# One attention and gated feed-forward kernel: a unit's scores and its attention outputs each gathered in one place, and the keys of batch 1 turned by a DMA

## The chip, the core and the metric

The kernel runs on one core of a Trainium2 chip, in one launch. The core has five engines with queues of their own: PE (TensorE, the matmuls; PEld are its weight loads), DVE (VectorE), ACT (ScalarE), POOL (GpSimd) and SP (SyncE, which only issues DMAs here). POOL issues DMAs too: those that convert float32 to bfloat16 on the way. The metric is the device time of one execution in microseconds (us), as the median of several runs; lower is better.

## The reference, cut to what matters

Two layers follow each other. The first is attention in which a query sees the keys closer than 16 positions and, beside them, 24 block summaries: the maximum over 32 keys and the mean over 32 values.

```python
batch, n_heads, seq, head_dim = (4, 8, 768, 64)
block, window = (32, 16)
k_sum = k.reshape(B, H, nb, block, D).max(axis=3)
v_sum = v.reshape(B, H, nb, block, D).mean(axis=3)
mask_l = np.abs(pos[:, None] - pos[None, :]) < window
scores_l = where(mask_l, scale * q @ k.T, -1e9)
scores_s = scale * q @ k_sum.T + log(block)
a = softmax(concat([scores_l, scores_s]))
attn = a @ concat([v, v_sum])
```

The second is a gated feed-forward layer on the 3072 rows of 512 that come out, with 1536 hidden columns:

```python
ffn_out = (gelu(x @ w_gate) * (x @ w_val)) @ w_out
out = x + sigmoid(x @ w_res) * ffn_out
```

## The kernel before, in words

The order of all instructions is written out by hand; each engine runs its own in that order, and semaphores are put in where data passes between engines or a buffer is used again.

**Units.** The work is cut into NU = 8 units u of 384 rows: batch b = u // 2, half = u % 2. The 8 heads go in 4 pairs hp. A unit has 6 tiles t of 64 queries; a tile's 64 + 32 neighbouring keys and the 24 block maxima stand side by side as 128 columns of `kW`, so that one 64-row matmul per tile and head gives all its scores, keys on the partitions. The two heads of a pair lie on the upper and lower 64 partitions, so their matmuls run two at a time.

**Attention of a unit.** `s_step` (L322) makes 12 score matmuls of a pair into two banks of PSUM (L317), takes the exponent on ACT into a tile `P` (L337 when both banks come from the two-bank pool `ps_s`, else twice L334), and from unit 1 on multiplies by the mask on DVE (L341). `av_step` (L347) makes the 12 matmuls with the values (L355) into an `ao` bank, whose row sums come along as a 65th column; `av_end` (L371) divides on DVE (a reciprocal, L373, and a product, L375, into `xn`). `xn` is then turned into `xT`: by PE and a copy in the first two units (`xt_step`, L377), by a DMA transpose from SP for each of four column groups ko from unit 2 on (`xt_dma`, L384).

**Feed-forward of a unit.** For each of 12 blocks fo, `fo_step` (L406) has PE make `g` and `vv` (four matmuls each, L395), ACT the gelu (L400) and DVE the product `gvT` (L401). `fo_first` (L413) leaves ko = 3 of both to the end, so that the last turned group may come late; `fo_last_two` (L420) makes both `g` before both `vv`. Then for each of 3 row groups `res_step` (L429: four matmuls, L433, and a tanh), `ffn_step` (L438: twelve matmuls, L443) and `end_step` (L458: two DVE passes, L449 and L452, and a store from SP, L456).

**Where the two meet.** `first_out` (after unit 0) and `mid_out` (L616, after units 1 to 6) interleave the end of unit u with the attention of unit n = u + 1. `mid_out` has: scores of pairs 0 and 1; two `res_step`; 4 of 12 matmuls of `f` 0; values of pairs 0 and 1; scores of pairs 2 and 3; the other 8 matmuls of `f` 0 and 3 of `f` 1; values of pairs 2 and 3; the rest. So PE goes from large matmuls to 64-row score matmuls or 64-column value matmuls and back twice, and the score and value groups also follow each other directly once.

**PSUM.** Eight banks: `ps_mm` has four, taken in turn by `g`, `vv`, `r`, `f` and some score banks; `ps_s` two; `ps_t` and `ps_o` one each.

**Keys, queries and values of a batch.** Batch 0 has a path of its own. For batches 2 and 3, `load_k_nat` (L118) loads k by eight DMAs from POOL with rows on the partitions, `turn_k` (L130) turns all of it by one DMA transpose from SP into `kW`, `k_rims` (L243) copies the 32 neighbouring keys of each tile on POOL, and `k_blocks` (L234) makes the block maxima on DVE, one pair after each of the steps fo = 2 to 5 of the unit before. For batch 1, k comes by one DMA into `k_sb` (L89) and is turned on PE: `turn_all` (L227) makes 64 small transposes (L220) after step fo = 0 of unit 1, and `k_place` (L251) after fo = 0, 2, 4 and 6 copies a pair on ACT (L252) and makes its maxima and rims on DVE. In POOL's queue the loads of a batch stand as k, then v (`v_loads`, L105, eight DMAs), then q (`load_q_nat`, L125, six). SP turns q in two halves (`turn_q`, L134), of which the first serves the batch's first unit. `vsum_grp` (L286) sums blocks of values with 12 PE matmuls (L290), a copy on ACT and four small DMAs from POOL; POOL then spreads the means (`vsum_bc`, L299). For batch 1 it stands after step fo = 5 of unit 1. `v_rims` (L110) copies neighbouring values by two DMAs from SP.

Of the kernel before, what the change touches and what calls it, by code (L numbers as in the profile page):

```python
# [8 lines left out]
F32 = mybir.dt.float32  # L9
BF16 = mybir.dt.bfloat16  # L10
# [5 lines left out]
def kernel(  # L16
# [11 lines left out]
    nc = tc.nc  # L28
# [25 lines left out]
    wpool = ctx.enter_context(tc.tile_pool(name="wpool", bufs=1))  # L54
    qk = ctx.enter_context(tc.tile_pool(name="qk", bufs=1))
    work = ctx.enter_context(tc.tile_pool(name="work", bufs=3))
    ppool = ctx.enter_context(tc.tile_pool(name="ppool", bufs=4))
    upool = ctx.enter_context(tc.tile_pool(name="upool", bufs=2))
    ps_mm = ctx.enter_context(tc.tile_pool(name="ps_mm", bufs=4, space=bass.MemoryType.PSUM))
    ps_s = ctx.enter_context(tc.tile_pool(name="ps_s", bufs=1, space=bass.MemoryType.PSUM))  # L60
# [17 lines left out]
    q_nat = const.tile([128, NQ, DM], BF16, name="q_nat")  # L78
    vext = [const.tile([128, NT, H, VP], BF16, name=f"vext{i}") for i in range(2)]
    vsum = [const.tile([128, DM], BF16, name=f"vsum{i}") for i in range(2)]  # L80
    vpart = const.tile([128, DM], BF16, name="vpart")
    w_gate = wpool.tile([128, KO, DFF], BF16, name="w_gate")
    w_val = wpool.tile([128, KO, DFF], BF16, name="w_val")
# [55 lines left out]
    with tc.manual_schedule():  # L139
# [182 lines left out]
        def s_step(u, hp, st, banks=None, tiles=None):  # L322
            if tiles:
                s, banks = tiles, True
            elif banks:
                s = [p.tile([128, 512], F32, tag=tag, name="s") for p, tag in banks]
            else:
                s2 = ps_s.tile([128, 2, 512], F32, tag="s", name="s")
                s = [s2[:, hh] for hh in range(2)]
            s_mm(u, hp, [x[:, 0:TU] for x in s])  # L330
            P = ppool.tile([128, 2, HT, QT], BF16, tag="P", name="P")
            if banks:
                for hh in range(2):
                    nc.scalar.activation(P[:, hh].rearrange("p t q -> p (t q)"), s[hh][:, 0:TU], AF.Exp,  # L334
                                         scale=scale, bias=bias_t[:])
            else:
                nc.scalar.activation(P.rearrange("p a t q -> p a (t q)"), s2[:, :, 0:TU], AF.Exp,  # L337
                                     scale=scale, bias=bias_t[:])
            if u:
                Pf = P.rearrange("p a t q -> p (a t) q")  # L340
                nc.vector.tensor_mul(Pf, Pf, maskt.unsqueeze(1).to_broadcast([128, 2 * HT, QT]))  # L341
            st["P", hp] = P

        MM2 = ((ps_mm, "mm"),) * 2
        TO2 = ((ps_t, "t"), (ps_o, "ao"))
# [31 lines left out]
        def xt_step(u, ko, st, pool, tag, copy=nc.vector.tensor_copy):  # L377
            xp = pool.tile([128, TU], BF16, tag=tag, name="xp")
            for sub in range(NSUB):
                nc.tensor.transpose(xp[:, sub * 128:(sub + 1) * 128],  # L380
                                    st["xn"][:, ko, sub, :], ident[:])
            copy(st["xT"][:, ko, :], xp[:])

        def xt_dma(ko, st):  # L384
            nc.sync.dma_start_transpose(out=st["xT"][:, ko].rearrange("d (s k) -> d s k", k=128),
                                        in_=st["xn"][:, ko].rearrange("p s d -> p (s d)"))
# [6 lines left out]
        def gv_mm(ps, w, st, fo, kos):  # L393
            for ko in kos:
                nc.tensor.matmul(ps[:, 0:TU], w[:, ko, fo * 128:(fo + 1) * 128], st["xT"][:, ko, :],  # L395
                                 start=(ko == 0), stop=(ko == KO - 1), skip_group_check=True)

        def gv_end(gvT, fo, g, vv):
            ge = work.tile([128, TU], F32, tag="ge", name="ge")
            nc.scalar.activation(ge[:], g[:, 0:TU], AF.Gelu)  # L400
            nc.vector.tensor_mul(gvT[:, fo, :], ge[:], vv[:, 0:TU])  # L401

        def mm_tile(name):
            return ps_mm.tile([128, 512], F32, tag="mm", name=name)
# [13 lines left out]
            gv_end(gvT, 0, g, vv)  # L418

        def fo_last_two(st, gvT):  # L420
            g = [mm_tile("g"), mm_tile("g")]
            for i in range(2):
                gv_mm(g[i], w_gate, st, FO - 2 + i, range(KO))
            for i in range(2):
                vv = mm_tile("vv")
                gv_mm(vv, w_val, st, FO - 2 + i, range(KO))
                gv_end(gvT, FO - 2 + i, g[i], vv)

        def res_step(st, sub):  # L429
            ss = slice(sub * 128, (sub + 1) * 128)  # L430
# [117 lines left out]
        xt_step(0, 2, st, **t_turn)  # L548
        gv_part(0, 1)
        gv_mm(gv[1][0], w_gate, st, 1, (0, 1))  # L550
        xt_step(0, 3, st, **o_turn)
        gv_part(0, 2)
        gv_mm(gv[1][1], w_val, st, 1, (0, 1))
        gv_part(0, 3)
# [27 lines left out]
        def pool_after(x):  # L582
            nc.gpsimd.tensor_copy(gate2[:], x)
# [31 lines left out]

        def mid_out(u, st, gvT, nst):  # L616
            n = u + 1
            other = dict(pool=ps_t, tag="t")
            s_step(n, 0, nst)
            s_step(n, 1, nst, TO2)  # L620
            res_step(st, 0)
            res_step(st, 1)
            ffn_step(st, gvT, 0, 0, 4)
            av_step(n, 0, nst)
            xt_dma(0, nst)
            av_step(n, 1, nst, **other)
            xt_dma(1, nst)
            s_step(n, 2, nst)
            s_step(n, 3, nst, MM2)
            if n % 2 == 0:  # L630
                pool_after(nst["P", 3][0:1, 0, 0, 0:1])
                for i in range(2, 4):
                    vsum_bc(n // 2, 3 * i, 3 * i + 3, nc.gpsimd)
            ffn_step(st, gvT, 0, 4, FO)
            ffn_step(st, gvT, 1, 0, 3)
            av_step(n, 2, nst)
            xt_dma(2, nst)
            av_step(n, 3, nst, **other)
            xt_dma(3, nst)
            end_step(u, st, 0)  # L640
            ffn_step(st, gvT, 1, 3, FO)
            res_step(st, 2)
            end_step(u, st, 1)
            ffn_step(st, gvT, 2, 0, FO)
            end_step(u, st, 2)
# [9 lines left out]
        for u in range(NU):  # L655
            b, half = u // 2, u % 2
            nb = b + 1
            if half == 0 and nb == 1:
                k_sb[nb] = k_tile()
                load_k(nb, k_sb[nb], 0, 1)  # L660
                v_loads(nb)
                load_q_nat(nb)
            if u:
                gvT = upool.tile([128, FO, TU], BF16, tag="gvT", name="gvT")
            for fo in range(0 if u else 2, FO):
                if u == 0 and fo == 2:
# [24 lines left out]
                if half == 1 and nb < B:  # L691
                    if fo == 0:
                        v_rims(nb, 0, HT)
                        if nb > 1:
                            pool_after(st["xT"][0:1, KO - 1, 0:1])
                            load_q_nat(nb)
                    if fo == (5 if nb == 1 else 1):
                        turn_q(nb, 0)
                        turn_q(nb, 1)
                        vsum_grp(nb, ps_t, "t")  # L700
                        for i in range(2):
                            vsum_bc(nb, 3 * i, 3 * i + 3, nc.gpsimd)
                    if nb == 1:
                        if fo == 0:
                            tk = turn_all(k_sb[nb])
                        if fo in (0, 2, 4, 6):
                            hp = (2, 0, 1, 3)[fo // 2]
                            k_place(nb, hp, tk[hp])
                    elif 2 <= fo < 2 + NP:
                        k_blocks(nb, fo - 2)  # L710
            if u == NU - 1:
                last_out(u, st, gvT)
            else:
                nst = new_unit()
                (mid_out if u else first_out)(u, st, gvT, nst)
                st = nst

# [29 lines left out]
```

The softmax here doesn't subtract the row's maximum and nothing guards it: scores larger than these inputs give would overflow.

## Time and profile before

| what | value |
|---|---|
| median of 4 runs | 256.31 us (256.27 to 256.33) |
| the profiled execution | 256.28 us |
| span of its trace | 254.5 us |
| outside the span | 1.8 us |
| granted TensorE clock | 0.998 |
| `mid_out` of unit 2 in the trace, from the first score matmul to the next unit's first `g` | 98.04 to 110.63 us |

The profile is one execution. Its page gives each engine's busy time and share of the span, the chain of work that ended last (followed back from the last instruction, at each step to what released it), and groups of instructions by line, with what ended the idle time before them. The trace behind it also answers for a window of time: the chain in order, an engine's instructions (the timeline), or the instructions of one tile with the time from a DMA's issue to its landing. Times of matmuls in the chain are from the end of one to the end of the next; in the timeline they begin when the matmul begins. Now and then a matmul's record is missing.

### The profile page before, as it was taken

To read this page: it belongs to the slowest core of one execution; us is meant where nothing else is said; L and a number is where in the kernel's file an instruction comes from. 1 tells how busy PE (TensorE), PEld (TensorE's weight loads), DVE (VectorE), ACT (ScalarE), POOL (GpSimd) and SP (SyncE) were. 2 spreads that over 40 slices of the span, in tenths; PEclk is the share of its full clock that TensorE was granted. 3 is DMA by queue.
4 is the path that set the end of the run, shared out by engine and by line. 5 is a ranking of instruction groups with operands and counts; after the bars stand their busy time and mean duration, and the time that the engine had idled before them with its cause. 6 is when DMAs were issued, how large, how long until landed. Compare 5 with 4: busy or idle time off the path is not lost.

```text
span 254.5 us, 5847 instructions
## 1 busy us (share of the span) xinstructions
PE 246.3 (97%) x2303; PEld 139.6 (55%) x2328; DVE 158.7 (62%) x364; ACT 129.5 (51%) x216; POOL 97.1 (38%) x128
## 2 busy tenths in 40 slices
PE   6999999999999999999999999999999999999994
PEld 2676555565545655445545665445545665456544
DVE  6985796398667544858567544858567544854424
ACT  8885458366572337354572337354572337353320
POOL 8885542361606970374406970274404000000000
PEclk9999999999999999999999999999999999999999
DMA  5999999999404999289404999289604400230003
GB/s 80 177 181 197 197 205 207 175 176 221 64 19 120 156 149 161 50 148 183 105 18 117 167 158 148 49 151 175 109 18 117 96 3 0 50 139 0 3 1 124
DMA packets 98108, 29.34 MB, mean 115 GB/s; under 512 B 83225, under 2 KB 94945, under 8 KB 97985
## 3 DMA queue, kind: packets, MB, share of 16 engines
q0 software_dynamic: 68352, 14.76, 65.4%
q1 hardware_dynamic: 29728, 14.21, 24.5%
q8 instruction: 18, 0.29, 0.5%
q14 instruction: 10, 0.07, 0.1%
HBM read 29.36 MB, written 6.29 MB: 140 GB/s over the span
## 4 chain that ended last, share of the span: by engine, by line
PE 93%; DVE 5%; issue 2%; DVEq 0%
PE g L395 25%; PE vv L395 24%; PE f L443 23%; PE r L433 8%; PE s L317 3%; PE ao L355 3%; PE vs L282 1%; PE ao L367 1%; PE tp L220 1%; PE vs L290 1%; DVE ks L237 1%; PE xp L380 1%; DVE o L452 1%; DVE th L449 1%; PE gv L395 1%
## 5 line engine op out<-in xcount | busy, mean ns | idle before, releaser
L401 DVE TENSOR_TENSOR gvT<-ge,vv 128x384 bf16<-128x384 f32 x95 | 52.2, 552 | 48.1 <-PE vv L395 43.9
L400 ACT ACTIVATE ge<-g 128x384 f32<-128x384 f32 x95 | 46.6, 490 | 67.4 <-DVE gvT L401 34.8
L395 PE MATMUL g<-xT,w_gate 128*128 128x384 bf16 x380 | 78.0, 326 | 0.0
L395 PE MATMUL vv<-xT,w_val 128*128 128x384 bf16 x380 | 77.8, 326 | 0.0
L443 PE MATMUL f<-w_out,gvT 128*128 128x512 bf16 x262 | 62.7, 379 | 1.5 <-issue 1.1
L395 PEld LDWEIGHTS <-w_gate 128*128 128x128 bf16 x384 | 37.1, 98 | 26.2 <-issue 1.4
L395 PEld LDWEIGHTS <-w_val 128*128 128x128 bf16 x384 | 37.6, 98 | 24.7
L443 PEld LDWEIGHTS <-gvT 128*128 128x128 bf16 x276 | 25.7, 98 | 29.5
L107 POOL DMA_DIRECT2D vext<-in_v_dram x32 | 24.1, 778 | 16.1 <-DMA w_out<-in_moe_w_out_dram 5.6
L436 ACT ACTIVATE th<-r 128x512 f32<-128x512 f32 x24 | 13.5, 606 | 27.5 <-PE r L433 27.5
L449 DVE SCALAR_TENSOR_TENSOR th<-th,f 128x512 f32<-128x512 f32 (+2 forms) x26 | 16.6, 640 | 14.3 <-PE f L443 14.3
L433 PE MATMUL r<-w_res,xT 128*128 128x512 bf16 x88 | 22.7, 380 | 0.4
L341 DVE TENSOR_TENSOR P<-P,maskt 128x768 bf16<-128x768 bf16 x28 | 15.7, 562 | 11.2 <-ACT P L337 6.1
L302 POOL COPY vext<-vsum 32x1536 bf16<-32x1536 bf16 x12 | 17.2, 1463 | 12.1 <-DMA vsum<-vpart 12.0
L452 DVE SCALAR_TENSOR_TENSOR o<-th,xn 128x512 f32<-128x512 f32 (+2 forms) x26 | 18.2, 700 | 0.9
L375 DVE TENSOR_TENSOR xn<-ao,rz 128x384 bf16<-128x384 f32 x32 | 17.8, 558 | 1.1
L337 ACT ACTIVATE P<-s,bias_t 128x768 bf16<-128x768 f32 x17 | 15.3, 901 | 4.5 <-PE s L317 4.3
L127 POOL DMA_DIRECT2D q_nat<-in_q_dram x18 | 15.8, 905 | 0.9 <-issue 0.9
L334 ACT ACTIVATE P<-s,bias_t 128x384 bf16<-128x384 f32 x30 | 15.7, 579 | 0.0
L237 DVE TENSOR_REDUCE ks<-kW 128x24 bf16<-128x768 bf16 x16 | 15.1, 943 | 0.0
L433 PEld LDWEIGHTS <-xT 128*128 128x128 bf16 x96 | 8.8, 98 | 9.9
L373 DVE RECIPROCAL rz<-ao 128x6 f32<-128x6 f32 x32 | 6.1, 191 | 11.2 <-PE ao L355 10.3
(90 smaller groups left out, 186.5 us busy)
## 6 DMA issues: line engine op xcount, KB each, us to landing
out_dram<-o SPq DMA_DIRECT2D x23, 256.0 KB, 2.2
vext<-in_v_dram POOLq DMA_DIRECT2D x32, 96.0 KB, 6.6
q_nat<-in_q_dram POOLq DMA_DIRECT2D x18, 128.0 KB, 6.2
w_gate<-in_moe_w_gate_dram POOLq DMA_DIRECT2D x6, 256.0 KB, 8.7
w_val<-in_moe_w_val_dram POOLq DMA_DIRECT2D x6, 256.0 KB, 9.0
w_out<-in_moe_w_out_dram POOLq DMA_DIRECT2D x3, 512.0 KB, 14.3
k_nat<-in_k_dram POOLq DMA_DIRECT2D x16, 96.0 KB, 5.7
vext<-vext SPq DMA_DIRECT2D x6, 144.0 KB, 5.5
```

The lines of the kernel that those rows point to most:

```text
L107: nc.gpsimd.dma_start(out=vext[b % 2][0:QT, :, h, 0:D], in_=v[b, h].rearrange("(t p) d -> p t d", p=QT))
L127: nc.gpsimd.dma_start(out=q_nat[:, c].rearrange("p (h d) -> p h d", d=D), in_=q[b, :, c * 128:(c + 1) * 128, :].rearrange("h p d -> p h d"))
L237: nc.vector.tensor_reduce(out=ks.rearrange("d (t n) -> d t n", n=2), in_=kw[:, :, 0:QT].rearrange("d t (n w) -> d t n w", w=BLK), axis=myb ...
L302: eng.tensor_copy(vext[b % 2][96:128, lo:hi, :, 0:D], src)
L375: nc.vector.tensor_mul(xn, ao[:, :, :, 0:D], rz.to_broadcast([128, NSUB, 2, D]))
L395: nc.tensor.matmul(ps[:, 0:TU], w[:, ko, fo * 128:(fo + 1) * 128], st["xT"][:, ko, :], start=(ko == 0), stop=(ko == KO - 1), skip_group_ch ...
L400: nc.scalar.activation(ge[:], g[:, 0:TU], AF.Gelu)
L401: nc.vector.tensor_mul(gvT[:, fo, :], ge[:], vv[:, 0:TU])
L433: nc.tensor.matmul(r[:], st["xT"][:, ko, ss], w_res[:, ko, :], start=(ko == 0), stop=(ko == KO - 1))
L443: nc.tensor.matmul(st["f", sub][:], gvT[:, fo, ss], w_out[:, fo, :], start=(fo == 0), stop=(fo == FO - 1), skip_group_check=True)
L449: nc.vector.scalar_tensor_tensor(th[:, cs], th[:, cs], 1.0, f[:, 0:n], ALU.add, ALU.mult)
L452: nc.vector.scalar_tensor_tensor(o.rearrange("p (k d) -> p k d", d=128), th[:, cs].rearrange("p (k d) -> p k d", d=128), 0.5, x, ALU.mult, ...
```

## The change

Six edits:

1. A constant tile `p_all` for all four pairs of a unit takes the place of the four `P` buffers.
2. In `mid_out`, `s_all` makes the unit's 48 score matmuls in one place, at the head. They fill three pairs of banks completely (eight tiles each, whatever the pair of heads): two `ps_mm` banks, `ps_s`, and `ps_t` with `ps_o`. ACT takes the exponents as 512 columns four times and 2x512 once; DVE masks in six pieces of 512.
3. `av_all` makes the 48 value matmuls in one place, after `res_step` 0 and 1 and all of `f` 0, into `ps_t`, `ps_o` and the two banks of `ps_s`. `av_end` and `xt_dma` of the four pairs follow.
4. k of batch 1 is loaded like that of batches 2 and 3 (eight DMAs from POOL) and turned by one DMA transpose, which stands in SP's queue ahead of the stores of unit 0. The rims are made on POOL at fo = 5 of unit 1 and the block maxima on DVE after fo = 6 to 9. The 64 PE transposes and the ACT copies go.
5. `fo_last_two` writes its gelu steps ahead of the `vv` matmuls; each engine's own order stays as it was.
6. In unit 0 the last of the four turned groups is copied by DVE and not by ACT.

```diff
+    p_all = const.tile([128, 2, NP * HT, QT], BF16, name="p_all")
...
-            P = ppool.tile([128, 2, HT, QT], BF16, tag="P", name="P")
+            P = p_all[:, :, hp * HT:(hp + 1) * HT]
...
+        def s_all(u):
...
+            for i in range(3):
+                if i == 0:
+                    s = [ps_mm.tile([128, 512], F32, tag="mm", name="s") for _ in range(2)]
+                elif i == 1:
+                    s2 = ps_s.tile([128, 2, 512], F32, tag="s", name="s")
+                    s = [s2[:, hh] for hh in range(2)]
+                else:
+                    s = [p.tile([128, 512], F32, tag=tag, name="s") for p, tag in TO2]
+                for j in range(8):
+                    hp, t = divmod(8 * i + j, HT)
+                    tt = half * HT + t
+                    for hh in range(2):
+                        ps = slice(hh * 64, hh * 64 + 64)
+                        nc.tensor.matmul(s[hh][:, j * QT:(j + 1) * QT], kw[ps, tt, hp, :],
+                                         qt[ps, tt // 2, hp, (tt % 2) * QT:(tt % 2 + 1) * QT],
+                                         start=True, stop=True, skip_group_check=True)
+                js = slice(8 * i, 8 * i + 8)
+                m = maskt.unsqueeze(1).to_broadcast([128, 8, QT])
+                for hh in range(1 if i == 1 else 2):
+                    if i == 1:
+                        nc.scalar.activation(p_all[:, :, js].rearrange("p a j q -> p a (j q)"), s2[:], AF.Exp,
+                                             scale=scale, bias=bias_t[:])
+                    else:
+                        nc.scalar.activation(p_all[:, hh, js].rearrange("p j q -> p (j q)"), s[hh][:], AF.Exp,
+                                             scale=scale, bias=bias_t[:])
+                for hh in range(2):
+                    nc.vector.tensor_mul(p_all[:, hh, js], p_all[:, hh, js], m)
+
+        def av_all(u, st):
...
+            for hp in range(NP):
+                if hp < 2:
+                    pool, tag = TO2[hp]
+                    ao = pool.tile([128, NSUB, 2, D + 1], F32, tag=tag, name="ao")
+                else:
+                    if hp == 2:
+                        s2 = ps_s.tile([128, 2, 512], F32, tag="s", name="ao")
+                    ao = s2[:, hp - 2, 0:NSUB * 2 * (D + 1)].rearrange("p (s h d) -> p s h d", s=NSUB, h=2)
...
+                if hp != 2:
+                    for i in range(2 if hp == 3 else hp, hp + 1):
+                        av_end(i, st, aos[i])
+                        if u > 1:
+                            xt_dma(i, st)
...
-        xt_step(0, 3, st, **o_turn)
+        xt_step(0, 3, st, ps_o, "ao")
...
         def mid_out(u, st, gvT, nst):
             n = u + 1
...
+            s_all(n)
...
             res_step(st, 0)
             res_step(st, 1)
...
+            ffn_step(st, gvT, 0, 0, FO)
+            av_all(n, nst)
             end_step(u, st, 0)
-            ffn_step(st, gvT, 1, 3, FO)
+            ffn_step(st, gvT, 1, 0, FO)
             res_step(st, 2)
...
-                k_sb[nb] = k_tile()
-                load_k(nb, k_sb[nb], 0, 1)
+                k_nat = load_k_nat(nb)
                 v_loads(nb)
                 load_q_nat(nb)
...
+                    if nb == 1 and fo == 5:
+                        k_rims(nb, slice(0, NP), nc.gpsimd)
                     if fo == (5 if nb == 1 else 1):
                         turn_q(nb, 0)
                         turn_q(nb, 1)
...
-                    if nb == 1:
-                        if fo == 0:
-                            tk = turn_all(k_sb[nb])
-                        if fo in (0, 2, 4, 6):
-                            hp = (2, 0, 1, 3)[fo // 2]
-                            k_place(nb, hp, tk[hp])
-                    elif 2 <= fo < 2 + NP:
-                        k_blocks(nb, fo - 2)
+                    lead = 6 if nb == 1 else 2
+                    if lead <= fo < lead + NP:
+                        k_blocks(nb, fo - lead)
...
                 nst = new_unit()
+                if u == 0:
+                    turn_k(nb, k_nat)
                 (mid_out if u else first_out)(u, st, gvT, nst)
```

More of the change, by code (lines that the diff above doesn't have):

```diff
@@ L56 @@
     work = ctx.enter_context(tc.tile_pool(name="work", bufs=3))
-    ppool = ctx.enter_context(tc.tile_pool(name="ppool", bufs=4))
     upool = ctx.enter_context(tc.tile_pool(name="upool", bufs=2))
@@ L339, in s_step @@
             if u:
-                Pf = P.rearrange("p a t q -> p (a t) q")
-                nc.vector.tensor_mul(Pf, Pf, maskt.unsqueeze(1).to_broadcast([128, 2 * HT, QT]))
+                nc.vector.tensor_mul(P, P, maskt.unsqueeze(1).unsqueeze(1).to_broadcast([128, 2, HT, QT]))
             st["P", hp] = P
+        def s_all(u):
+            b, half = u // 2, u % 2
+            kw, qt = kW[b % 2], qT[b % 2]
+            s2 = None
+            for i in range(3):
[25 more added lines that the diff above has]
+                    nc.vector.tensor_mul(p_all[:, hh, js], p_all[:, hh, js], m)
@@ new lines, in av_all @@
+        def av_all(u, st):
+            b, half = u // 2, u % 2
+            aos = []
+            for hp in range(NP):
[6 more added lines that the diff above has]
+                    ao = s2[:, hp - 2, 0:NSUB * 2 * (D + 1)].rearrange("p (s h d) -> p s h d", s=NSUB, h=2)
+                for sub in range(NSUB):
+                    for hh in range(2):
+                        for e in range(2):
+                            t = 2 * sub + e
+                            nc.tensor.matmul(ao[64 * e:64 * e + 64, sub, hh, :], p_all[:, hh, hp * HT + t, :],
+                                             vext[b % 2][:, half * HT + t, 2 * hp + hh, 0:D + 1],
+                                             start=True, stop=True, skip_group_check=True)
+                aos.append(ao)
+                if hp != 2:
[3 more added lines that the diff above has]
+                            xt_dma(i, st)
@@ L420, in fo_last_two @@
         def fo_last_two(st, gvT):
-            g = [mm_tile("g"), mm_tile("g")]
+            ge = []
             for i in range(2):
-                gv_mm(g[i], w_gate, st, FO - 2 + i, range(KO))
+                g = mm_tile("g")
+                gv_mm(g, w_gate, st, FO - 2 + i, range(KO))
+                ge.append(work.tile([128, TU], F32, tag="ge", name="ge"))
+                nc.scalar.activation(ge[i][:], g[:, 0:TU], AF.Gelu)
             for i in range(2):
@@ L426, in fo_last_two @@
                 gv_mm(vv, w_val, st, FO - 2 + i, range(KO))
-                gv_end(gvT, FO - 2 + i, g[i], vv)
+                nc.vector.tensor_mul(gvT[:, FO - 2 + i, :], ge[i][:], vv[:, 0:TU])
         def res_step(st, sub):
@@ L617, in mid_out @@
             n = u + 1
-            other = dict(pool=ps_t, tag="t")
-            s_step(n, 0, nst)
-            s_step(n, 1, nst, TO2)
+            s_all(n)
+            if n % 2 == 0:
+                pool_after(p_all[0:1, 1, 4 * HT - 1, 0:1])
+                for i in range(2, 4):
+                    vsum_bc(n // 2, 3 * i, 3 * i + 3, nc.gpsimd)
             res_step(st, 0)
             res_step(st, 1)
[L623 to L639, printed above, removed]
+            ffn_step(st, gvT, 0, 0, FO)
+            av_all(n, nst)
             end_step(u, st, 0)
-            ffn_step(st, gvT, 1, 3, FO)
+            ffn_step(st, gvT, 1, 0, FO)
             res_step(st, 2)
```

## The prediction

> **What bounds the kernel now.** I read the page's busy shares first, then the chain that ended last, then the chain piece by piece where the change cuts in.
>
> ```profile
> PE 246.3 (97%) x2303; PEld 139.6 (55%) x2328; DVE 158.7 (62%) x364; ACT 129.5 (51%) x216; POOL 97.1 (38%) x128
> ...
> PE 93%; DVE 5%; issue 2%; DVEq 0%
> ```
>
> PE is busy for 97% of the span and makes 93% of the chain; DVE's 5% lies almost all in the start. So an edit gains what it takes out of PE's stream, and loses where PE begins to wait. The chain in unit 1, around the 64 small transposes:
>
> ```profile
> 52.45 0.65 PE vv L395 x4
> 53.09 1.48 PE tp L220 x64
> 54.58 0.76 PE g L395 x4
> 55.33 0.65 PE vv L395 x4
> ```
>
> And through `mid_out` of unit 2 (the columns are start, length, what):
>
> ```profile
> 98.04 0.46 PE s L317 x24
> ...
> 100.33 0.86 PE f L443 x4
> 101.19 0.50 PE ao L355 x24
> 101.69 0.46 PE s L317 x24
> 102.14 0.16 issue
> 102.30 2.32 PE f L443 x10
> 104.62 0.50 PE ao L355 x24
> 105.12 2.05 PE f L443 x9
> ...
> 110.63 0.16 PE g L395
> ```
>
> The reader is to see two things: the transposes stand alone on the path, and each time the kind of matmul changes, the first group after it is longer than its matmuls: nine `f` take 2.05 where four take 0.86, that is 0.216 each and 1.94 for nine.
>
> **The transposes of batch 1 go.** Without them the `g` after 53.10 would end at 53.75 and not at 55.33: 55.33 - 53.10 - 0.65 = 1.58 us off the path.
>
> **Fewer changes of kind, six times.** The stretch takes 110.63 - 98.04 = 12.59 us. Its contents at their steady pace: 48 large matmuls (12 `r`, 36 `f`) at 0.216 are 10.37. In the timeline 24 score matmuls show 0.52 us busy at 0.19 each, so 23 steps take 0.33: 0.34 for 24, 0.69 for 48. Likewise 24 value matmuls, 0.57 at 0.195: 0.39, so 0.78 for 48. Together 11.84. The other 0.75 belongs to seven changes (vv-s, s-r, f-ao, ao-s, s-f, f-ao, ao-f): 0.107 each. The 0.16 of "issue" is an unrecorded matmul and a change, not a wait: 0.16 + 2.32 is eleven `f` (2.37) and 0.11. Afterwards four changes are left (vv-s, s-r, f-ao, ao-f), so three go: 0.32 per unit, 1.93 for units 1 to 6.
>
> **What hides the rest of the new order** (in the clock of unit 2). PE: scores 98.0 to 98.75, two `r` of 0.86 to 100.5, `f` 0 of 2.59 to 103.1, values from 103.2 to 104.0. ACT's table load ends at 98.56 as before. Its exponents are 901 ns for 768 columns and 572 for 384, starts 0.80 and 0.46 apart: 0.875 ns a column and 0.13 fixed, so 0.58 for 512 and 1.02 for 1024, 3.3 in all (before 3.4), the last done at 102.0. A mask product is 0.56 for 768 columns; 512 cost between 0.37 (in proportion) and 0.56, I take 0.43, and the last ends about 102.45. Cover: 0.7 us to PE's first `ao`, more to the last pair. If it goes, PE waits one for one, at most some 0.3 by these ends. The `r` banks wait for ACT until 103.2, and PE wants them back at 106.9. The rest (merged `P`, order of `fo_last_two`) moves nothing in any engine's order: 0.
>
> **What is late next: the turned `xn`.** All four `xt_dma` now start after 103.2, where two started at 102.48 before.
>
> ```profile
> 102.48 5.80 SPq L385 DMA_TRANSPOSE xT<-xn  x4
> ```
>
> From its first `ao` (104.55) to SP's third issue (105.80) it took 1.25, so the first issue comes at 104.43. SP spends 1.2 on each, the first 1.2 to 1.8, and a small gap: the fourth is issued at 108.2 to 108.85 and lands 2.3 later (tile view), at 110.5 to 111.15. DVE, at 0.7 per pair, is no slower. The next unit's `g` moves to 110.3 at the chain's clock and wants ko = 3 after six matmuls of 0.16, at 111.1 in matmul starts. So it costs 0 to 0.15 per unit; I take 0.2 for six.
>
> **Unit 0's copy by DVE.** ACT's 478 ns copy lets `g` start at 23.02, 0.08 after its slot; DVE's row of the same shape is 357 ns and DVE is idle there: -0.08.
>
> **Batch 1's DMA chain**, which replaces the transposes. POOL's rows first:
>
> ```profile
> 30.06 1.00 POOL L89 DMA_DIRECT2D k_sb<-in_k_dram  x1 [0.57 <-DMA w_val<-in_moe_w_val_dram]
> ...
> 45.08 0.74 POOL L107 DMA_DIRECT2D vext<-in_v_dram  x1 [1.78 <-DMA w_out<-in_moe_w_out_dram]
> 48.98 0.75 POOL L107 DMA_DIRECT2D vext<-in_v_dram  x1 [3.16 <-DMA k_sb<-in_k_dram]
> 50.82 4.38 POOL L127 DMA_DIRECT2D q_nat<-in_q_dram  x5 [0.22 <-issue]
> ```
>
> By the tile view the last w_out lands at 44.8 (16.1 after its issue at 28.7), k at 48.7 (18.6 after 30.06), the eight v loads by 54.2 (the last 5.2 after 48.98): 5.5 us for eight loads of 128-byte packets. k as eight loads has v's form, so it lands at 50.3. Then SP issues the transpose, as it did twice for later batches:
>
> ```profile
> 94.12 5.35 SPq L131 DMA_TRANSPOSE kW<-k_nat  x1
> ```
>
> The page's list of DMA issues has the time to landing as its last column:
>
> ```profile
> kW<-k_nat SPq DMA_TRANSPOSE x2, 8.5
> ```
>
> There, too, v loads were under way: the last v, issued at 94.69, landed 8.0 later against 5.2 in unit 1. So kW is there 8.3 to 8.7 after 50.3, about 58.8, and the last v about 58.7, 4.5 later than before. Three waits follow:
> - PE's sums of values begin at 61.1 - 1.6 = 59.5 and need every v: 0.8 to spare.
> - DVE's first maxima come after fo = 6, about 62.1: 3.3 to spare. Each is 0.95 + 0.23 behind a 0.55 product; batches 2 and 3 carry the same four in four steps without a gap on PE.
> - PE's scores at 69.8 - 1.6 = 68.2 need the first half of q. Its three loads were there at 56.4 (tile view); they shift by 4.5 and up to 1.5 more for the stores and rims that now fall into them: 61 to 62.5. The turn takes 4.7 to 6.3 (tile view, unit 1): 65.7 to 68.8.
>
> SP's queue has the transpose ahead of unit 0's three stores, which go out 3 us later; their buffers are wanted again after 75. POOL's rims (0.77 to 1.19 each, two) stand ahead of the four `vsum` DMAs (0.5 each) and two spreads (1.46 each): 62 + 2 + landing 3 to 5.4 + 2.9 gives 70 to 72.3, and values of unit 2 are wanted about 73.4. I take 0 to 0.6 for these waits, and 0.1 in the sum.
>
> [...]
>
> **The sum.** 256.28 - 1.58 - 1.93 - 0.08 + 0.2 + 0.1 = 252.99 for the profiled execution; its median is 0.03 higher, so **253.0**.
>
> **Rivals.**
> - *A: batch 1's DMAs put a wait where the transposes were* (v at 59.5, or q at 68.2). For: margins of 0.8 and about 1 out of landings that vary by 1.6. Against: the same queue order in two later batches. Price 0.5 to 2: 253.5 to 255.0. Chance 0.24.
> - *B: `mid_out` gives its gain back* in a wait of `ao` for the last mask products, or of `g` for the fourth turned group. For: 0.7 and 0 us of cover. Price 0.1 to 0.32 in each of six units: 253.4 to 254.9. Chance 0.13.
> - *C: slower than before.* The transpose is served only behind the queued v and q loads and kW lands after 66.5. DVE then stands at the first maxima with the products behind it, `vv` banks stay full and PE stops: from 62.5 on, a us of lateness costs a us, and the gain of 3.3 and the 0.5 of the bound are gone at 66.3. For: unit 1 is where the DMA engines are fullest (nine tenths to the 64th us in the page's slices). Against: both later transposes got through beside v. 257 to 259. Chance 0.05.
> - *That it doesn't do what it says*: a change of kind costs less when 48 small matmuls follow each other (the 0.107 is a mean). Then 0.5 to 1 of the 1.93 is lacking: 253.5 to 254.0. Chance 0.06.
>
> **How the numbers follow.** My forecast, 252.4 to 253.4, has 0.52. A measurement of this kernel tells 0.2% (0.51 us) from no change; the forecast, A, B and the last rival lie below 255.77 but for a tail, which with the overlap of A and B (both prices paid) I put at 0.06 for no change. So faster 0.89, same 0.06, slower 0.05. The range 252.3 to 255.2 takes in A, B and the bounds of the unknown costs; it leaves out C, the tail and a little below.
>
> **What would show it.** No `tp` at 53 in the chain, and steps of 0.65 through it. In `mid_out`: 48 `s` and 48 `ao` in one piece each, 12.27 us from `s` to `g`, no idle PE before `ao`; the fourth `xT` landing near the next `g`. In unit 1: kW landing about 59, no PE gap at `vs` (59.5) or at the first `s` (68.2). Wrong if PE shows idle time ended by a DMA of vext, qT or xT, or if DVE stands before the first maxima.

## The result, and the profile after

| | before | after |
|---|---|---|
| median | 256.44 us (62 runs, 256.09 to 259.76) | 256.85 us (44 runs, 255.79 to 259.32) |
| the profiled execution | 256.28 us | 257.02 us |
| its span | 254.5 us | 254.6 us |
| outside the span | 1.8 us | 2.4 us |

The ratio after to before is 1.0021, with a 95% interval of 1.0011 to 1.0031: slower by 0.2%, where 253.0 us (1.3% faster) was forecast. The prediction was wrong, and 256.85 lies above its range as well.

Busy time fell as planned. These are the first line of busy times on the page of after, and its line with the engines' shares of the chain that ended last:

```profile
PE 243.7 (96%) x2245; PEld 138.0 (54%) x2264; DVE 159.3 (63%) x369; ACT 124.7 (49%) x205; POOL 103.9 (41%) x137
...
PE 66%; DMA 24%; POOL 5%; DVE 2%; issue 2%; SPq 0%; POOLq 0%; DVEq 0%
```

PE is busy 2.6 us less than before, and yet the span is the same. The chain was PE at 93%; now DMAs have 24% of it. Their part ends at unit 2's scores: followed back from there, the chain runs through q's turn and load and POOL's queue to the loads of the weights in unit 0. From the chain of after (start, length, what):

```profile
45.95 5.97 POOL vext L107 x8
...
53.58 10.84 DMA q_nat<-in_q_dram
...
64.51 6.08 DMA qT<-q_nat
...
70.72 0.88 PE s L360 x48
```

The 64 transposes are gone from it (no `tp` stands at 53). In their place the chain has a load of q and then q's turn, for which PE waits. The list of what PE waited for in after has these rows, none of which the same list of before has:

```profile
PE s L360 <- DMA qT<-q_nat: 1.9, 1, 1.9
...
PE g L451 <- DMA xT<-xn: 0.5, 1, 0.5
...
PE g L451 <- DVE th L508: 0.2, 1, 0.2
...
PE vs L290 <- DMA q_nat<-in_q_dram: 0.2, 1, 0.2
```

(Columns: us in total, times, longest.) Ends of matmuls are modelled, so I count waits by the starts of matmuls in the timeline. In unit 1 there are three:

- The first `g` after the place of the transposes begins at 53.29, 1.02 after the `vv` ahead of it; groups of four follow each other by 0.65. That is a wait of 0.37 for the bank of an `f`, which DVE's second `th` of unit 0 reads until 53.23. In before that `th` ends at the same time (53.24), and the transposes cover it.
- `vs`, the sums of values, begins at 60.12, 0.96 after the `vv` ahead of it, against 0.74 in before: a wait of 0.22. The last v landed at 59.67. The list names q here; that it is v's is read from experiments 3 and 8, where the last v lands at 59.35 and 55.05: they have the first wait and not this one.
- Scores of unit 2 begin at 70.72, where 68.8 was possible: 1.93.

SP's queue in after shows why q's turn is late (start, length, what):

```profile
50.12 5.96 SPq L131 DMA_TRANSPOSE kW<-k_nat  x1
56.13 1.55 SPq L515 DMA_DIRECT2D out_dram<-o  x3
...
64.51 6.20 SPq L136 DMA_TRANSPOSE qT<-q_nat  x2
```

SP is free from 61.2 on; the turn waits for q's third load, which lands at 64.42 (56.42 before). The transpose of k was issued at 50.12 and landed at 61.05, 10.9 us later.

`mid_out` did what was forecast. From the chain of after, through unit 2's:

```profile
98.66 0.81 PE s L360 x48
...
103.88 0.88 PE ao L390 x48
...
109.96 2.35 DMA xT<-xn
...
112.34 0.32 PE g L451
```

Scores and values stand in one piece each, with no wait ahead of the values. From the first score to the next unit's first `g` it takes 12.16 or 12.17 us in after, by starts, against 12.49 or 12.50 before in the same places. The last two lines are the other new wait: the fourth `xT` lands at 112.30, and `g` is held up behind it.

### The profile page after: what moved, and what is told of

It is laid out like the page before. It is cut to its first block, busy times and chain, and to the rows that moved or that the text cites. A ratio compares the mean times of both kernels' runs of the same rounds, so it can differ in the third digit from the quotient of the medians.

```text
span 254.6 us, 5737 instructions
## 1 busy us (share of the span) xinstructions
PE 243.7 (96%) x2245; PEld 138.0 (54%) x2264; DVE 159.3 (63%) x369; ACT 124.7 (49%) x205; POOL 103.9 (41%) x137
## 4 chain that ended last, share of the span: by engine, by line
PE 66%; DMA 24%; POOL 5%; DVE 2%; issue 2%; SPq 0%; POOLq 0%; DVEq 0%
PE g L451 18%; PE f L502 18%; PE vv L451 18%; PE r L492 7%; DMA w_out<-in_moe_w_out_dram 6%; DMA q_nat<-in_q_dram 4%; DMA w_val<-in_moe_w_val_dram 4%; DMA vext<-in_v_dram 3%; DMA qT<-q_nat 2%; POOL vext L107 2%; DMA k_sb<-in_k_dram 2%; PE ao L390 2%; PE s L360 2%; DMA xT<-xn 2%; DVE th L508 1%
## 5 line engine op out<-in xcount | busy, mean ns | idle before, releaser
L456 ACT ACTIVATE ge<-g 128x384 f32<-128x384 f32 x81 | 39.8, 491 | 64.9 <-DVE gvT L457 33.2
L457 DVE TENSOR_TENSOR gvT<-ge,vv 128x384 bf16<-128x384 f32 x81 | 44.4, 552 | 39.2 <-PE vv L451 36.0
L502 PE MATMUL f<-w_out,gvT 128*128 128x512 bf16 x268 | 61.9, 379 | 1.2 <-issue 1.1
L121 POOL DMA_DIRECT2D k_nat<-in_k_dram x24 | 18.2, 788 | 10.3 <-DMA w_out<-in_moe_w_out_dram 5.7
L373 DVE TENSOR_TENSOR p_all<-p_all,maskt 128x512 bf16<-128x512 bf16 x36 | 15.2, 455 | 9.0 <-ACT p_all L370 5.8
L511 DVE SCALAR_TENSOR_TENSOR o<-th,xn 128x512 f32<-128x512 f32 (+2 forms) x26 | 16.9, 651 | 0.9
L370 ACT ACTIVATE p_all<-s,bias_t 128x512 bf16<-128x512 f32 x24 | 15.3, 692 | 1.8 <-PE s L360 1.8
```

The costliest lines, as they stand in the source:

```text
L121: nc.gpsimd.dma_start(out=k_nat[:, :, h * D:(h + 1) * D], in_=k[b, h].rearrange("(t p) d -> p t d", p=QT))
L502: nc.tensor.matmul(st["f", sub][:], gvT[:, fo, ss], w_out[:, fo, :], start=(fo == 0), stop=(fo == FO - 1), skip_group_check=True)
L511: nc.vector.scalar_tensor_tensor(o.rearrange("p (k d) -> p k d", d=128), th[:, cs].rearrange("p (k d) -> p k d", d=128), 0.5, x, ALU.mult, ...
```

## The experiments

Each kernel was timed beside the kernel before on the same chip (256.41 to 256.52 us in the four sets). Two letters stand for theories in the first four expectations: D, that the losses are waits for batch 1's DMAs (edit 4), and G, that waits for `xT` come from POOL's gate, which opens k's loads only when the last `xT` is there.

**1. The new middle part alone** (edit 4 undone; called kernel 1 from here on).

```diff
-                k_nat = load_k_nat(nb)
+                k_sb[nb] = k_tile()
+                load_k(nb, k_sb[nb], 0, 1)
...
+                            tk = turn_all(k_sb[nb])
...
-                    turn_k(nb, k_nat)
```

> All edits but the fourth: the keys of batch 1 come by one DMA and are turned on PE as before. Theory D (the DMA chain of batch 1 gives back what its edit saves and more: waits of 0.6 us for v and 1.9 us for q against 1.58 us saved; mid_out saves 0.32 us in each of six units, less some 0.8 us of waits for the last turned xT): faster than before by 1.0 to 1.6 us, so about 254.9 to 255.4 us, no PE wait at the sums of values or at the first scores of unit 2. Theory M (the new order of mid_out is what eats the gain): within 0.4 us of before or slower.

254.63 us (254.51 to 254.93), ratio 0.9927 [0.9914, 0.994]. From its chain:

```profile
97.76 0.81 PE s L360 x48
...
102.99 0.88 PE ao L390 x48
...
110.02 0.49 PE g L451 x3
```

Only matmuls stand between these, back to back: `g` comes 12.26 after the scores, on the chain's clock. PE does not wait at `vs` or at the first scores, and waits for `xT` once (0.2). So edits 1 to 3, 5 and 6 are worth 1.8 us, 0.2 more than the most that was expected, and theory D has its first half.

**2. Edit 4 alone**, in the kernel before.

> The kernel before with the fourth edit alone (k of batch 1 as eight loads, one DMA transpose, rims on POOL, maxima at fo = 6 to 9); mid_out as before. Theory D: slower than before by 0.6 to 1.3 us (2.5 us of waits against 1.58 us saved), about 257.0 to 257.7 us, with PE waiting at the sums of values and at the first scores of unit 2. Theory M: faster by 0.5 to 1.6 us.

257.5 us (257.1 to 259.6), ratio 1.0049 [1.0016, 1.0082]: slower. PE's waits:

```profile
PE s L317 <- DMA qT<-q_nat: 2.0, 1, 2.0
...
PE vs L290 <- DMA q_nat<-in_q_dram: 0.7, 1, 0.7
```

The two waits are those of after, in a kernel with the old middle part; the one for DVE's `th` is there too. (The profile is of an execution of 259.6 us, so they are a little longer than in after.) Taking 1.58 us of transposes off PE cost more than 2.7 us of waits in it, and the time is in the range expected. D holds.

**3. The second half of q later** (after, with batch 1's last three loads of q behind the sums of values).

```diff
-                load_q_nat(nb)
+                load_q_nat(nb, range(NSUB))
...
+                            load_q_nat(nb, range(NSUB, NQ))
+                            turn_q(nb, 1)
```

> The changed kernel with one difference: of the queries of batch 1, the second half (needed only by unit 3) is loaded behind the four small sums-of-values DMAs and no longer ahead of them. Theory D (the first half's turn is slow because the other half's loads run beside it): the turn takes 4.4 us or less in place of 6.1, the wait at the first scores of unit 2 falls from 1.9 us to 0 to 0.6, the wait for v stays at 0.6, and the time is 1.2 to 1.9 us below the changed kernel. Rival: the turn is late because the first half's own loads land late (64.4), and takes as long without the others: the wait stays above 1.2 us and the time within 0.7 us of the changed kernel.

257.1 us, ratio 1.0006 [0.9988, 1.0024]: not to be told from before, nor clearly from after. In the profiled execution the wait at the scores is 1.3, not 1.9: the turn lands 5.4 after its issue, but the first half's own third load still lands at 64.34. (The list names POOL's spread for this wait, which ends at 69.95; the turn lands at 69.86.) So the second half of q takes 0.6 us of the wait; the rest stands ahead of it. Of the expectation the rival's terms hold: a wait above 1.2 and a time within 0.7 us of after.

**4. POOL's gate on the first `xT`** (kernel 1, with `pool_after` on ko = 0 instead of the last, in both of its places for later batches).

```diff
-                    pool_after(st["xT"][0:1, KO - 1, 0:1])
+                    pool_after(st["xT"][0:1, 0, 0:1])
```

> As e1_mid_only, and POOL's gate for the loads of batches 2 and 3 looks at the first turned column group (ko = 0) and not at the last. Theory G (the later xT releases the k loads later, their transpose then runs into the next unit's xT transposes, and that is the 0.6 us wait of PE in unit 3): 0.4 to 0.9 us faster than e1_mid_only, kW of batch 2 landing 3 to 4 us earlier. Rival: the loads now run beside the other three xT transposes and make them land later: the same as e1_mid_only or slower, with PE waits for xT in units 2 and 3.

263.97 us (262.33 to 264.7), ratio 1.0288 [1.0265, 1.0312]: 9 us slower than kernel 1. PE's waits for `xT`, and the chain where the first stands:

```profile
PE g L451 <- DMA xT<-xn: 7.9, 5, 2.3
```

```profile
80.14 5.12 DMA xT<-xn
```

With loads of k under way, the `xT` transpose took 5.12 us to land, not 2.3. G falls: opening the gate sooner is the costliest edit of all. It also shows the trouble of edit 4 on a smaller scale: beside these loads, of 128-byte lines, the transpose took 2.2 times as long.

**5. and 6. Batch 1's loads in another order**: k, half of q, v (5), and half of q with its turn ahead of k, then v (6). In both the sums of values come after fo = 8. The lines are those of 5.

```diff
-                k_nat = load_k_nat(nb)
-                v_loads(nb)
-                load_q_nat(nb)
+                k_nat = load_k_nat(nb)
+                load_q_nat(nb, range(NSUB))
+                v_loads(nb)
+                load_q_nat(nb, range(NSUB, NQ))
```

> The changed kernel with batch 1's loads in another order: k, the first half of q, v, the second half of q; the turn of q's first half is issued ahead of the rims of v, the sums of values and the turn of q's second half come after fo = 8 instead of 5. My theory: the changed kernel loses its 1.58 us of transposes because v and q land late beside the 0.79 MB transpose of k, and the losses are 0.58 us at the sums of values and 1.9 us at the first scores of unit 2. With q's three loads directly behind k they should land near 55, the turn be issued when SP is done with k's (56.1) and land at 62 to 64, before the scores want it (68.2); v lands near 62 to 64.5, the sums want it at 63.4. Then both waits go but for 0 to 1 us, and the run takes 253.0 to 254.3. Rival 1: the turn of q is slow because it stands behind k's turn on the same queue whatever the loads do: lands after 66, less than 1 us is won: 256 or more. Rival 2: the sums of values come too late for the spreads by POOL, a wait at the first value matmuls of unit 2 of 1 to 2 us takes the place: 255 to 256.

> As the one before, but with the first half of q loaded and turned ahead of k. q's loads land near 47.5, its turn is issued at once and lands before 55; k lands near 52.5, its turn is issued near 53 to 54 and kW lands at 62 to 65, v near 62 to 64.5. The first maxima (62.1) can be 3.3 us late before PE stands. Theory: no wait at the scores of unit 2, 0 to 1 us at the sums of values, 253.0 to 254.5. Rival: k's turn stands behind q's on the queue and kW comes after 66: a wait at the scores through the maxima, 255 to 257.

258.88 us (ratio 1.0096 [1.0065, 1.0127]) and 261.09 us (1.0172 [1.0155, 1.0189]): my theory missed in both. In 5, q's third load landed at 52.44, as hoped, but its turn took 10.5 (59.02 to 69.53) and the last v landed at 67.45, as its chain shows:

```profile
53.93 13.52 DMA vext<-in_v_dram
```

The sums were to begin at 63.4. (PE was 3.2 us late already in this execution, with a granted clock of 0.50 in unit 0, from 20 to 26 us, so only 0.6 shows as a wait.) Rival 1's terms came true, a landing after 66 and 256 us or more; its reason, the place behind k's turn on the queue, is not shown. In 6, q was turned at 55.72, but kW landed at 66.61, the maxima on DVE came late, and PE stood 2.5 us behind DVE's products. In each of the two orders what was put last was late; neither of them helps.

**7. The values in two places again** (kernel 1, with `av_all` for pairs 0 and 1 after `f` 0, for 2 and 3 after three matmuls of `f` 1).

> The kernel with the new middle part and the old batch 1 (254.6 us before), with the value matmuls of a unit in two places again: head pairs 0 and 1 after the first f, 2 and 3 after three matmuls of the second. Theory (each change of kind on TensorE costs 0.107 us): two more changes a unit, 12.17 becomes 12.38 us, six times 0.214 is 1.28: 255.6 to 255.9. Rival: most of the 0.33 us came from the scores in one piece, or from longer runs of small matmuls: under 0.6 in all, 254.6 to 255.2.

255.91 us (255.74 to 256.15): 1.2 to 1.3 above kernel 1, as expected. Two more changes of kind in each of six units cost 1.2 to 1.3 us, 0.10 to 0.11 each. In its trace `mid_out` of unit 2 takes 12.39 by starts, where 12.38 was expected, and PE has no wait that kernel 1 has not. The rival falls.

**8. k's transpose later** (after, with `turn_k` issued after fo = 3 of unit 1, behind the rims of v).

```diff
-                if u == 0:
-                    turn_k(nb, k_nat)
...
+                    if nb == 1 and fo == 3:
+                        turn_k(nb, k_nat)
```

> The changed kernel with the transpose of k of batch 1 issued after fo = 3 of unit 1, behind the rims of v, so that v and the first half of q are loaded without it. Theory: the transpose slows these loads; without it v is there near 54 to 55 (59.7 in the changed kernel) and q's first half near 57 to 58 (64.4), and PE does not wait at the sums of values. kW lands at 65 to 67 and the turn of q behind it at 67 to 70, so waits come at the maxima, the rims and the values of unit 2 instead, and the run takes 257 to 260. Rival: the loads are late without the transpose too (v after 58, q after 62); then something else slows them.

261.94 us (1.0228 [1.0194, 1.0262]), 2 us above the range expected. It is there for its landings: the last v at 55.05 (59.67 in after), as expected, q's third load at 59.56 (64.42), later than the 57 to 58 expected. So the transpose is most of what slows these loads, and something else takes some 3 us of q's (56.37 in kernel 1). kW lands at 67.43; PE then stands 2.8 us behind DVE and 1.2 behind the maxima.

**9. and 10. Half of k by DMA, half on PE**; in 10 with the second half of q later, as in 3.

```diff
+            nc.gpsimd.dma_start(out=k_nat[:, 0:HT, h * D:(h + 1) * D],
+                                in_=k[b, h, 0:TU].rearrange("(t p) d -> p t d", p=QT))
+        k_half = k_tile()[:, :, 0:QJ]
...
+                            tk = turn_all(k_half)
```

> The changed kernel with batch 1's k turned in halves: the first six tiles of 64 keys by a DMA transpose of 0.39 MB, the last six by 32 transposes on TensorE (loaded as lines of 512 bytes) with their copies by ScalarE; rims and maxima as in the changed kernel. My theory: the whole transpose of 0.79 MB is too much for the DMA engines between the 45th and the 70th us, in whatever order, and half of it is not. Loads of k are done near 48, half of kW lands near 53 to 55, v near 57 (TensorE wants it at 60.3), q's first half near 60, its turn at 65 to 67 (wanted at 69.0). No waits, and half of the 1.58 us gained: 253.6 to 254.2, about 0.8 below the kernel with the new middle part alone. Rival: any transpose by DMA there slows q and its turn past 69.5; then at least 0.5 to 1.5 us of wait: 254.5 to 256.

> The half-and-half kernel with the second half of batch 1's q loaded behind the sums of values (it is wanted only by unit 3). Where a wait for q's turn is left at the first scores of unit 2, this takes up to 0.6 us of it, as it did in the changed kernel; where none is left, the same time as the half-and-half kernel within 0.3 us.

258.24 us (1.0074 [1.0044, 1.0104]) and 259.7 us (1.0114 [1.0072, 1.0157]): both missed, and the theory that half the bytes would be half the trouble fell. From the chain of 9:

```profile
57.61 7.13 DMA q_nat<-in_q_dram
...
64.76 6.62 DMA qT<-q_nat
```

Half a transpose landed 9.7 us after its issue (the whole one 10.9), the last v at 62.18, and PE waited 2.1 at the sums of values. Half the lines of k are still small ones, and SP's issue took 1.43 and not 5.96, so that the stores of unit 0 went out at 52.64 and not 56.13, among the loads of v. How these share the loss wasn't tried. In 10 the wait at the scores is gone, but the one at the sums of values stays (2.0), and turned `xn` costs 1.7 in five places.

**11. Kernel 1 again.**

> The kernel with the new middle part and the old batch 1 once more, beside the two others on the same chip: 254.4 to 254.9.

254.71 us (254.48 to 254.96), ratio 0.9919 [0.9889, 0.9949]. It is the version that beats both kernels, shown twice.

**12. and 13. Small lines without the transpose, and the transpose without small lines.** Kernel 1 with k loaded as in after (lines of 128 bytes, where kernel 1 has 1024) but turned on PE from there (12), and kernel 1 with one more transpose of 0.79 MB of which nobody reads the result (13).

```diff
-                k_sb[nb] = k_tile()
-                load_k(nb, k_sb[nb], 0, 1)
+                k_nat = load_k_nat(nb)
...
-                            tk = turn_all(k_sb[nb])
+                            tk = turn_nat(k_nat)
```

```diff
+            nc.vector.tensor_copy(spare[:, 0, 0:1], nst["xn"][:, 2, 0, 0:1])
             av_step(n, 3, nst)
+            nc.sync.dma_start_transpose(out=spare,
+                                        in_=w_gate[0:QT].rearrange("p k f -> p (k f)"))
```

> The kernel with the new middle part and the old batch 1, but with k of batch 1 loaded as in the changed kernel (eight loads of 128-byte lines instead of one load of 1024-byte lines) and turned by TensorE from there (48 transposes of 64 x 128). No DMA transpose of k. If the transpose is what makes v and q late, v is there near 55, q's first half near 57.5 and its turn before 65; TensorE does not wait, and the time is 254.2 to 254.9. If the small lines make them late, v is there after 57, q's first half after 60.5 and the turn after 67, and up to 1 us of waits comes: 255 to 256.

> The kernel with the new middle part and the old batch 1 (k in one load of 1024-byte lines, turned by TensorE), with one more DMA transpose of the size of k's, 0.79 MB, of which nobody uses the result: it is issued near 50, turns a part of w_gate and writes it into a spare tile. If the transpose alone makes v and q late, v is there after 58 (53.9 without it), q's first half after 61 (56.4 without), the turn of q after 68, and TensorE waits 0.5 to 3 us in unit 1: 255.1 to 257.7. If it is the small lines of k, v and q are less than 1.5 us later than without it and the time is 254.5 to 255.

254.98 us (254.8 to 255.45) and 255.3 us (254.76 to 255.76). Landings in the profiled executions, in us:

| | last v | third load of q | turn of q issued | landed | wait at the scores |
|---|---|---|---|---|---|
| kernel 1 (neither) | 53.91 | 56.37 | 57.39 | 63.79 | 0 |
| 12 (small lines) | 55.32 | 62.20 | 62.28 | 67.58 | 0 |
| 13 (transpose) | 58.78 | 62.88 | 62.90 | 70.38 | 0.6 |
| after (both) | 59.67 | 64.42 | 64.51 | 70.59 | 1.9 |

The chain of 13 ends in the same two DMAs as that of after:

```profile
51.59 11.30 DMA q_nat<-in_q_dram
62.90 7.48 DMA qT<-q_nat
```

(The transpose of 13 was issued at 48.06, 2 us earlier than k's in after.) Each alone makes q's loads some 6 us late; only the transpose makes v late by 5, the small lines by 1.4. They don't add up (8.0 for q with both). The expectation for 12 was half wrong: v lands early as with the transpose at fault, q late as with the lines at fault. The wait of 13 is 0.6 where after has 1.9, though q lands at nearly the same time in both: in 13 PE still makes its 64 transposes and comes to the scores later.

## Why the prediction was wrong, point by point

- **The PE transposes (-1.58): 1.21 of it was there.** The sum took them to stand alone on the path. But the `g` behind them begins at 53.29, where 52.92 would be its place, because DVE's `th` of unit 0 still holds its bank: 0.37 of what the transposes took was cover. What DVE still does there was put at nothing, though its rows in the trace of before show it. The wait is in the list of each version without PE transposes in unit 1 (after, experiments 2, 3, 5, 6 and 8), and in none with them.
- **Three fewer changes of kind (-1.93): right.** 0.32 to 0.34 in each of six units, 1.98 in all; experiment 7 puts two of them back and pays 1.2 to 1.3.
- **What hides the new order: right.** The last mask product of unit 2 begins at 103.08 and the first `ao` at 103.81; no wait. Unit 0's copy gave its 0.08.
- **Turned `xn` late (+0.2): too small in after.** `g` waited 0.62 and 0.22 in the starts of units 3 and 4. In kernel 1 it is 0.40 in one profile and nothing in the other (experiment 11), so most of it comes with edit 4. Ahead of unit 3's start SP's third issue took 2.1 us and not 1.2, and kW of batch 2 had landed at 106.29 (102.82 before): its transpose was issued 0.5 later and took 11.7 us and not 8.7. That the one comes from the other is argued and not shown.
- **Batch 1's DMA chain (+0.1): this step failed.** It took the landing of kW from two later batches (8.3 to 8.7, really 10.9), v's from there as well (58.7, really 59.67), and let q's three loads shift by 4.5 and up to 1.5 more. They shifted by 8.0. The turn's own 4.7 to 6.3 was right (6.1). So 65.7 to 68.8 became 70.6, and the two waits, for v and for q's turn, cost 0.22 + 1.93 = 2.15 us where 0.1 was in the sum. The error behind it: the later batches load no q and store nothing beside k's transpose and v, and there k had 128-byte lines before the change as well. In unit 1 the edit adds the transpose and the small lines to a stretch in which q and the stores run too; experiments 12 and 13 show that each delays q by some 6 us. Nor was 8.3 to 8.7 a fixed figure: the same transpose took 10.5 for batch 2 in kernel 1 and 11.7 and 11.1 in the later batches of after, beside v alone, with two or three loads of v issued behind it where before has one. And the DMA engines were busy for 90% or more of the time there already (a 9): the page's slices of DMA (6.4 us each), before and after, show it.

```profile
DMA  5999999999404999289404999289604400230003
```

```profile
DMA  5999999999942999759902999759703600140003
```

  Before, the full stretch ends in the eleventh slice (4 from 63.7 us on); after, that slice is 9 and the twelfth is 4. The 64 transposes stand in the trace of before as matmuls on PE (1.48 us, L220), with no DMA among them.
- **The rivals.** A came true, with 2.15 us where its price was 0.5 to 2, and of B the part of the turned groups, with 0.84 in all; both at once had been left in the tail. C's mechanism is real, but its place wasn't reached: kW landed at 61.05 and DVE was in time. Experiments 6 and 8 reach it (66.61 and 67.43), and there PE stands 2.5 and 2.8 us behind DVE.
- **What no step had.** The last stores cost 0.35 (an issue of 0.81 instead of 0.33 us, and PE's earlier end is lost), PE's start is 0.07 later, and 0.60 us lies outside the span.

The sum as it was, for the profiled executions: 256.28 - 1.58 - 1.98 - 0.08 + 0.37 + 0.22 + 1.93 + 0.84 + 0.35 + 0.07 + 0.60 = 257.02; measured 257.02. (To the hundredth this is luck: each term is read to some 0.01 or 0.02.)

## What to carry to other kernels

Work that was moved from a full engine to the DMAs was not free here: 1.58 us came off PE, and 2.15 us of waits came back from a stretch whose slices of DMA stood at 90% or more. Ask whether the DMA engines have time between the last load that is under way and the first that is wanted; read the slices of the stretch in which the work will run, not those of a later repeat of the loop that looks alike. Each load behind the new transfer must be moved in the estimate: here, with the transpose in flight for 10.9 us and k in small lines, q's third load came 8.0 later and the last v 5.5. What an edit takes off the path was also cover for others (0.37 us here): ask what the step behind it waits for once it comes sooner. And gather small matmuls of one kind into one run: each change of kind cost PE 0.10 to 0.11 us here, with runs of 24 as with runs of 48.

## What the runs showed of the hardware that was not expected

**Behind waits of 2.0 to 2.8 us the granted clock fell to 0.50, in some executions or in all.** In experiment 6 PE stands for 2.5 us to 68.74; then the granted clock goes down (columns: window, its length, busy us of PE, PEld, DVE, ACT and POOL with instructions, granted clock, DMA share, GB/s):

```profile
69.00:70.00 1.00, 1.00 (x6) 0.49 (x4) 0.97 (x3) 0.00 (x0) 1.00 (x3) 0.66 0.44 59
...
71.00:72.00 1.00, 1.00 (x4) 0.45 (x3) 0.97 (x4) 0.47 (x1) 0.00 (x0) 0.50 0.93 209
...
73.00:74.00 1.00, 1.00 (x22) 0.53 (x21) 1.00 (x1) 1.00 (x1) 1.00 (x1) 1.00 0.00 0
```

PE runs at half its clock for some 3.4 us, and matmuls of 0.16 take 0.32: 1.7 us are lost. In experiments 6 and 8 (waits of 2.5 and 2.8) all ten executions have a mean clock of 0.993 or less. With waits of about 2 us it is some: 5 of 12 in experiment 9, and 2 of 9 in experiment 2, where they took 259.6 and the others 257.4; in the profiled one the granted clock is 0.50 from 72 to 75 us, directly behind the wait of 2.0. In after, with 1.9, it is 4 of 44, at 258.7 to 259.3, which is the upper end of its scatter. Not each of these need come from the wait: the kernel before has no such wait in unit 1, and 2 of its 61 executions beside the experiments have clocks of 0.986 and 0.987, at 259.3. In the profiled executions of experiments 2, 6 and 8 the slow stretch begins, by the windows, within some 0.6 us of the wait's end and is 3.4 us long each time; that the wait sets it off, and what ends it, is not shown.

**Time outside the span.** It is 1.77 us (median) before, 2.01 in kernel 1, 1.89 in experiment 2, and 2.39 in after. Experiments 3, 5, 6 and 8, made from after, have 2.38 to 2.45 too; 9 and 10, with half of k on PE, have 2.04 and 2.02. So all of after's loss in the medians (0.4) lies where the profile shows nothing; by the spans alone (median 254.5 in after, 254.6 to 254.8 for the kernel before in the four sets) it is not slower. Its cause stays open.

**An issue of a DMA transpose was not in proportion to its size.** SP was held for 5.96 us by 0.79 MB in after and for 1.43 by half of it in experiment 9; the size is not all of it, since the same 0.79 MB held it for 5.21 in the last batch of before and for 6.13 in experiment 13.

**Beside a copy on POOL a mask product on DVE took 2.8 to 3.8 times as long.** In after the product at 71.87 takes 1.61 us instead of 0.42, while POOL spreads block means (70.33 to 73.2); in experiment 2 the one at 72.72, of 768 columns, takes 1.59 instead of 0.56 beside the same copy. It had cover. What ties the two together is not shown.
